# A big transposing weight load taken out of the head of a fused attention and gating kernel, with a newly searched engine order

## The chip, the cores and the metric

The kernel runs on one core of a Trainium2 chip. Times are device microseconds (us) of one execution. A run profiled by the hardware has a span, some 1.7 us shorter than its time. All runs told of here were in the fast state, at a granted TensorE clock of 0.99 to 1.00. Ratios are computed from the means: the mean time of one kernel's fast runs over that of the other's of the same rounds, so they are not quite the ratio of the medians quoted.

## The reference, cut to what matters

Two blocks on x of shape [1, 2048, 512] in bfloat16. The first is a linear attention with 32 heads, the second a gated MLP that mixes along the sequence with a 2048 x 2048 "spatial" matrix w_sp.

```
phi = lambda t: jnp.where(t > 0, t + 1, jnp.exp(t)) + 1e-06
q, k, v = split(layernorm(x) @ wqkv);  pq, pk = phi(q), phi(k)
o = (pq @ (pk^T v)) / (pq . sum(pk) + 1e-06)
h = x + o @ wo
z = gelu(layernorm(h) @ w_in);  z1, z2 = halves of z
g = w_sp @ layernorm(z2) + b_sp
out = h + (z1 * g) @ w_out
```

The matter here is the first 18 us: sixteen tiles of 128 rows of x are loaded, normalised, transposed and multiplied with the key weights. Tiles 0 to 5 are transposed by TensorE, tiles 6 to 15 by a transposing DMA on the SP queue. w_sp is needed transposed, from 118 us on.

In the kernel and its views xn is the normalised x and xnT its transpose, hn and hnT are the same for h, pk is phi(k), the z sum is the sum of pk over the rows, and wsp is w_sp transposed. x4 is the load of tiles 4 and 5, x6 that of tiles 6 and 7, and so on. SPq stands for SP's queue: the time beside it is how long an issue holds SP. The time to landing runs from the start of the issue until the data are there.

## The kernel before

The program records every operation with its dependencies; a packed string ORDER then gives the order in which each engine runs them. The loads of the head, on the two issuing queues SP and ACT:

```python
x0 = load_x("SP", 0, 1, 2150)
load_x("ACT", 1, 1, 2250)
x2 = load_x("SP", 2, 1, 2500)
load_x("ACT", 3, 1, 2500)
wk = [first_load(eng, wqkv[:, c:c + 2, D:2 * D], ...) for eng, c in (("SP", 0), ("ACT", 2))]
for n, lat, behind in ((4, 2000, x2), (6, 2200, x2), (8, 1900, wk[0]), (10, 2100, wk[0]), (12, 2300, wk[0]),
                       (14, 2500, wk[0])):
    load_x("SP", n, 2, lat, behind)          # two tiles; "behind": SP waits until that load has landed
first_load("SP", wqkv[:, :, 0:D], A_wqkv[:, 0:D], "wq", 3400)
```

The tiles from 6 on, and the spatial loads, of which the first EARLY ones are whole and stand ahead of the first transposed tile of x (cuts are marked with ...):

```python
# in k_unit(n), for i in (n, n + 1), n >= HEAD = 6
norm("ACT", xn[:, i, :], x[:, i, :], ...)
g.last = dma_t(xnT[:, :, i * P:(i + 1) * P], xn[:, i, :], f"xt{i}")   # transposing DMA on SP
...
for i, t in enumerate(order):                       # 16 row blocks of w_sp
    w = NT // 2 if EARLY <= i < NT // 2 else NT     # halves, or the whole block
    for j in range(0, NT, w):
        op = dma_t(wsp[:, j:j + w, t * P:(t + 1) * P], B_w_sp[t * P:(t + 1) * P, j * P:(j + w) * P], ...)
        ...
        if i < EARLY:
            first_xt.soft.add(op.i)                 # the load goes ahead of the first transposed tile
```

Of the kernel before, what the change touches and what calls it, by code (L numbers as in the profile page):

```python
# [8 lines left out]
ACT = mybir.ActivationFunctionType  # L9
ALU = mybir.AluOpType  # L10

P = 128
GRAN = 16
EARLY = 1
SEM_NS = 45.0
ORDER = "c-jTQ17HvU00h8Cwq47%ZQHhO+qGrewr$(CZ5wwH5gAbt9Wf9Su@D<^5Eu2800D@ED2Rr5$b~$}jl4*LqyUHz2nE3iiC_qhWJrz_NQp#9j8w>n{3w9JNQ(-ngvO|hifD@XNQl%(gMui6bjW~0NROh(gp4SL;;4eE$c!dvhAgOttSEtOsEO>Tj&A6I?kI_#D23)|fpBPrmgt4v=!-tcfm*16wy2FdXpPdSi+UJ`GAN7sXn-*oi}6^7B{+=bSc-PYiE=294rqh+XoyA_fPol{e&~-u=!i}@g3dUILzsYxn1sn#foYh6Ay|pf2#+ubi&cn#)i{b{IDz9BieU)ENCaUNMq>@uVLGOw3%X(^W?%v4<1|iU78YVH*5eGG;uKz@fg0)sp5qy2V-AL61U6tJ7GW`VU^_NpGqzwZ=3x)^VkdTCH_qWK_F+E`U@Nxa3a;WjF5n_A;U+HQ8gAh_Zr~N(;5FXjHtypN?&2OEA~+u)1Vi#2BJdF+G7{h8F`nQjKHvvF;uk*QAHLu-zTqprBPPMH49!ps!&o$9Gb*DoGNUja<1-H9G91J6H)1dqQ!@`UGdlA!3-hx8(=aX5F+DRdBQvoaOS2ZqeEfr~EJ*P$$}kwSF*|cGCkwGWb1{GkSeQjvl*L$=3Au#z*pj)~gSA<lCE13Fn3xr~m}Oa?OIe4l*qXiBmVH=}l~|co*p6$smJQgDjaZfK*^@Qcm`&J=eVLTWS%RgQgvq#t$(4dlnUc-9hbgp-TbWvEG@MgdjoUbaBiWA~*pZ#sp99#L138Gxxt%+>f-5<d={22=)L1pSjx(4+d%2HY*p1EDg4LN)sgzl1704hC<zRMaR}SM4Hc=L(Q$~$qCQai^o?%vHQ+DN0PUTiE<y9W#S3VU`K^0aZ713E9VR02z2^CXml~fs(S1Fa%9UkQ|-sKg(;Z>H?6TW2y&EkF@;6bkE25#hNj^S92<4*44A&%#4&f#3H;yg~^ah~9OF63cO;wEn9J>KU7KIBQB;yb?Q2cF}3Uf@OU=4r0xHD2c>HdQk<R|~aND^2DCPUIq1RAp7tA3o(X{$&+a)fawcHHBAeB~u%<RXep;2X#~@bygR3RRn!waD`A!g;Xtl<a6HOO+MlazT_>w;wS!NL|x`<J|+}NRAhbU5B}sY-e!CyP!xqyXh~rdRbgcXD4~8ckrFG3s;h>gD~3KZreZ0!!YP`PDvshRnBr-G`e?9ftFC6Kj%I3zhN_+hs;_2ixVmYIrfQJ7tG{|^l~!w-rYle*HCMybQzO(*qclz%G+MnBr16@ddFrkC8lzd7sC8PPC0eMpO5(Aaqyw6xrCOuOTBh~dsLfiWE!wJs+NPvltP@(U?b@Xk+N71*p}jh+L)xvK+Nb?GqCGmQ<4Wk0I;GP(qeMQY#LnfjI;RvquM4`QD@y5$itl8;rcb)A54x<Yx}&?grJK5^+`g{|O6>#=@JBt;L#6U#J<|(4(Nm@MXT8=drE_{e*B8CiS7q=!z125;*AFFk7XQ*uW%O_T6a7bjmEXZ^!*XbcabAaX2#0lehjSWda#m+{HWzR~M{q<(avn!@WJh-t7jkw-a|{=DKF4t^$8-+obP*SIF_&>!7k3HQbA88kBR6&vH*hmIbxD_ULr-!GH+OlrbSw9A8~1h}w{}IBb|qK#1o!hq_jP{{a67kkdk^#=5AiTp@nBbVIoEInS95jObS>9*M|bu{*Ku8UcMnhTR8MmUZ}Mgj^(+r}Cy(?DPxlsg@np|*kViPsvpvsqJl6}n$V)um3%%G&J<g-u)nmQfqrA+kywYpD*6SSG!F@yV+|!}F)$jF2x7E#KyxJ=~-s`==+q~U7ywkh<AMVe{ZU"


class _Op:
# [233 lines left out]
def bass_sequential_preLN__linear_attn_block__mixer_gmlp__prompt_kernel(  # L253
# [11 lines left out]
    _, S, D = A_x.shape  # L265
    F = B_w_in.shape[1]
    FH = F // 2
    H = 32
# [9 lines left out]
    g = _Prog(nc)  # L278
# [41 lines left out]
    x = g.sbuf("x", o_x, [NT, D], BF16)  # L320
    h = g.sbuf("h", o_x, [NT, D], BF16)
    xn = g.sbuf("xn", o_xn, [NT, D], BF16)
    wqkv = g.sbuf("wqkv", o_wqkv, [KD, 3 * D], BF16)
# [4 lines left out]
    pk = g.sbuf("pk", o_pk, [NT, D], BF16)  # L328
# [146 lines left out]
    def first_load(eng, dst, src, nm, lat, behind=None):  # L475
        q = queue[eng]
        op = load(eng, dst, src, nm, lat)
        op.bias = 1e6
        if q:
            op.soft.add(q[-1].i)  # L480
        if behind is not None:
            op.deps.add(behind.i)
        q.append(op)
        return op

    def load_x(eng, n, w, lat, behind=None):
        return first_load(eng, x[:, n:n + w, :], x_d[n * P:(n + w) * P, :], f"x{n}", lat, behind)

    x0 = load_x("SP", 0, 1, 2150)
    load_x("ACT", 1, 1, 2250)  # L490
    x2 = load_x("SP", 2, 1, 2500)
    load_x("ACT", 3, 1, 2500)
    wk = [first_load(eng, wqkv[:, c:c + 2, D:2 * D], A_wqkv[c * P:(c + 2) * P, D:2 * D], f"wk{c}", 3500)
          for eng, c in (("SP", 0), ("ACT", 2))]
    for n, lat, behind in ((4, 2000, x2), (6, 2200, x2), (8, 1900, wk[0]), (10, 2100, wk[0]), (12, 2300, wk[0]),
                           (14, 2500, wk[0])):
        load_x("SP", n, 2, lat, behind)
    first_load("SP", wqkv[:, :, 0:D], A_wqkv[:, 0:D], "wq", 3400)
    exp_table = g.add("ACT", lambda ac: ac.preload_act_table_set("natural_log_exp_and_others"), [], [], cost=1300)
    exp_table.soft.add(queue["ACT"][-1].i)  # L500
    exps = []
# [12 lines left out]
    def rstd(s, r, n, w, col, neg, sign=1.0):  # L514

        rr, ss = r[:, n:n + w, :], s[:, n:n + w, :]
        pool(lambda p: p.tensor_scalar(rr[:, :, 1:2], ss[:, :, col + 1:col + 2], sign, EPS_LN, op0=ALU.mult,
                                       op1=ALU.add), [ss[:, :, col + 1:col + 2]], [rr], 230)
        pool(lambda p: p.tensor_tensor(rr[:, :, 0:1], rr[:, :, 1:2],  # L519
                                       expo[:, 0:w].rearrange("p (a b) -> p a b", b=1), ALU.pow), [rr, expo], [rr],  # L520
             620 + 120 * (w - 1))
        if neg:
            for i in range(n, n + w):
                pool(lambda p, i=i: p.tensor_scalar(r[:, i, 2:3], s[:, i, col:col + 1], r[:, i, 0:1], -1.0,
                                                    op0=ALU.mult, op1=ALU.mult), [r[:, i, :], s[:, i, :]], [r[:, i, :]], 240)

    def rstd_act(s, r, n, w, col):
        rr, ve = r[:, n:n + w, :], s[:, n:n + w, col + 1:col + 2]
        act_exp(rr[:, :, 1:2], ve, ACT.Ln, 80, bias=epst[:, 1:2], extra=[epst[:, 1:2]])
        act_exp(rr[:, :, 0:1], rr[:, :, 1:2], ACT.Exp, 80, scale=-0.5)  # L530
# [22 lines left out]
    def norm(eng, dst, src, s, r, n, col, w):  # L553
        mean, rst, nmr = s[:, n, col:col + 1], r[:, n, 0:1], r[:, n, 2:3]
        if eng == "DVE":
            return dve(lambda v: v.tensor_scalar(dst, src, mean, rst, op0=ALU.subtract, op1=ALU.mult), [src, mean, rst],  # L556
                [dst], w + 460, acc=4)
        elif eng == "ACT":
            act(dst, src, ACT.Identity, w, bias=nmr, scale=rst, extra=[nmr, rst])
        else:  # L560
            pool(lambda p: p.tensor_scalar(dst, src, rst, nmr, op0=ALU.mult, op1=ALU.add), [src, nmr, rst], [dst],
                 200 + 1.5 * w)
# [43 lines left out]
    def next_pair():  # L606
        pc[0] += 1
        return PAIRS[pc[0] % 2]

    CB, first_xt, second = [4, 5, 6, 7], None, None  # L610
    HEAD, SINGLE = 6, 4
    ACTS = (1,)
    QSPLIT, KSPLIT, CACT = (6, 7), (), 2


    def k_unit(n):
        nonlocal first_xt, second
        b = next_pair()
        for i in (n, n + 1):
            if i in ACTS:  # L620
                s = st[0][:, i, :]
                act(sh_t[0], x[:, i, :], ACT.Identity, D, accum=s[:, 0:1])
                act(sh_t[1], x[:, i, :], ACT.Square, D, scale=D ** -0.5, accum=s[:, 1:2])
                moments(s, 6, D)
                rpow(s[:, 7:8], rs[0][:, i, 0:1])
            else:
                op = stats(x, 0, i)
                if i == 0:
                    second = warmup(16, 60, op)
                if n == 0:  # L630
                    rstd_act(st[0], rs[0], i, 1, 6)
        if n == 2:
            rstd_act(st[0], rs[0], n, 2, 6)
        elif n:
            rstd(st[0], rs[0], n, 2, 6, n >= HEAD)
        for i in (n, n + 1):
            norm("DVE" if n < HEAD else "ACT", xn[:, i, :], x[:, i, :], st[0], rs[0], i, 6, D)
            if n < HEAD:
                pe_transposes(xn[:, i, :], b + i % 2, xnT, i, second)
            else:  # L640
                g.last = dma_t(xnT[:, :, i * P:(i + 1) * P], xn[:, i, :], f"xt{i}")
                if i == HEAD:
                    first_xt = g.last
        for i in (n, n + 1):
            matmuls(bank(b + i % 2), [(xnT[:, c, i * P:(i + 1) * P], wqkv[:, c, D:2 * D]) for c in range(KD)])
        if n < SINGLE:
            for i in (n, n + 1):
                phi(pk[:, i:i + 1, :], b + i % 2, 1)
        else:
            phi(pk[:, n:n + 2, :], b, 2, n in KSPLIT)  # L650

        def fn(pe, i):
            inst = None
            for c in range(KD):
                inst = pe.matmul(bank(CB[c]), lhsT=xn[:, i, c * P:(c + 1) * P], rhs=pk[:, i, :],  # L655
                                 start=i == 0, stop=i == NT - 1)
            return inst
        for i in (n, n + 1):
            PE(lambda pe, i=i: fn(pe, i), [xn[:, i, :], pk[:, i, :]], [bank(b) for b in CB], KD * 216)
# [67 lines left out]
    for c in range(KD):  # L727
        b = CB[1 - c % 2]
# [100 lines left out]
    k = 0  # L829
# [190 lines left out]
```

## Time and profile before

| | before |
|---|---|
| median time, first three runs | 233.2 us (232.9 to 233.53) |
| profiled span | 231.8 us |
| TensorE busy | 224.6 us (97%) |
| first matmul on a tile transposed by DMA | 18.58 us |
| TensorE's wait for that tile | 1.20 us |

TensorE is the bound nearly everywhere, so only its gaps are worth looking for, and the lines that the prediction shows lead to the one at 17.4 to 18.6 us. Two more lines are of use. They end the views of the tiles wsp and xnT of the kernel before, and give the time from issue to landing, first for the spatial loads, then for the transposes of x:

```profile
DMA to landing us min/median/max: 3.4/4.9/9.1
```

```profile
DMA to landing us min/median/max: 2.4/2.5/4.1
```

The longest of the first, 9.1 us, is the load in the head: issued at 8.86, landed at about 17.96 us. The longest of the second is tile 7, issued at 14.47 and landed at 18.53.

### The profile page before, as it was taken

To read this page: it belongs to the slowest core of one execution; us is meant where nothing else is said; L and a number is where in the kernel's file an instruction comes from. 1 tells how busy PE (TensorE), PEld (TensorE's weight loads), DVE (VectorE), ACT (ScalarE), POOL (GpSimd) and SP (SyncE) were. 2 spreads that over 40 slices of the span, in tenths; PEclk is the share of its full clock that TensorE was granted. 3 is DMA by queue.
4 is the path that set the end of the run, shared out by engine and by line. 5 is a ranking of instruction groups with operands and counts; after the bars stand their busy time and mean duration, and the time that the engine had idled before them with its cause. 6 is when DMAs were issued, how large, how long until landed. Compare 5 with 4: busy or idle time off the path is not lost.

```text
span 231.8 us, 3231 instructions
## 1 busy us (share of the span) xinstructions
PE 224.6 (97%) x1180; PEld 112.1 (48%) x1203; DVE 161.6 (70%) x323; ACT 104.3 (45%) x193; POOL 44.2 (19%) x134
## 2 busy tenths in 40 slices
PE   8997999999999999999999999999999999999995
PEld 8543444453445443454544444444455555555452
DVE  4998755646987550237489989979795566785485
ACT  5694754399989876679862010101021211123010
POOL 3436300000466608023771000000000000000000
PEclk9999999999999999999999999999999999999999
DMA  5893259947546635968999700000000000020025
GB/s 182 263 214 70 59 138 230 315 147 181 114 89 136 117 71 121 183 126 188 185 228 197 159 3 0 0 0 0 3 0 1 0 3 0 20 72 3 0 80 191
DMA packets 58864, 23.68 MB, mean 102 GB/s; under 512 B 48480, under 2 KB 58720, under 8 KB 58848
## 3 DMA queue, kind: packets, MB, share of 16 engines
q1 hardware_dynamic: 58144, 22.88, 44.7%
q10 hardware_dynamic: 704, 0.59, 0.8%
q8 instruction: 9, 0.15, 0.3%
q14 instruction: 7, 0.06, 0.1%
HBM read 7.47 MB, written 2.10 MB: 41 GB/s over the span
## 4 chain that ended last, share of the span: by engine, by line
PE 86%; DMA 6%; ACT 3%; DVE 2%; issue 1%; SPq 0%
PE psum L402 70%; PE psum L802 6%; PE psum L655 5%; PE psum L805 4%; DMA x<-in_A_x_dram 3%; DMA xnT<-xn 2%; DMA hnT<-hn 1%; DVE st L511 1%; ACT sh L421 1%; ACT xn L421 1%; ACT e L421 0%; ACT xnT L421 0%; PE psum L751 0%; PE psum L676 0%; PE psum L720 0%
## 5 line engine op out<-in xcount | busy, mean ns | idle before, releaser
L421 ACT ACTIVATE psum<-psum 128x256 f32<-128x256 f32 (+1 forms) x33 | 14.3, 445 | 90.8 <-PE psum L402 63.1
L402 PE MATMUL psum<-wsp,z 128*128 128x512 bf16 x204 | 47.5, 379 | 0.2
L402 PEld LDWEIGHTS psum<-wsp,z 128*128 128x128 bf16 x208 | 20.4, 98 | 22.9
L402 PE MATMUL psum<-hnT,win 128*128 128x512 bf16 x108 | 25.6, 379 | 0.2
L421 ACT ACTIVATE e<-psum 128x1024 bf16<-128x1024 f32 (+1 forms) x18 | 16.7, 926 | 15.2 <-PE psum L402 14.3
L402 PE MATMUL psum<-t,s 128*128 128x512 bf16 x94 | 22.1, 379 | 0.1
L421 ACT ACTIVATE z1T<-psum 128x512 bf16<-128x512 f32 x28 | 16.6, 594 | 4.9 <-PE psum L402 4.8
L802 PE MATMUL psum<-win,hnT 128*128 128x512 bf16 x64 | 16.4, 379 | 0.4 <-DMA hnT<-hn 0.4
L402 PE MATMUL psum<-wout,z1T 128*128 128x256 bf16 (+1 forms) x82 | 16.6, 314 | 0.1
L402 PEld LDWEIGHTS psum<-hnT,win 128*128 128x128 bf16 x112 | 10.0, 98 | 13.2 <-ACT z1T L421 3.8
L402 PE MATMUL psum<-wqkv,xnT 128*128 128x512 bf16 x61 | 14.8, 380 | 1.4 <-DMA xnT<-xn 1.2
L421 ACT ACTIVATE z<-psum 128x896 bf16<-128x896 f32 x16 | 14.5, 909 | 2.9 <-PE psum L805 2.8
L402 PE MATMUL psum<-xnT,wqkv 128*128 128x512 bf16 x61 | 15.1, 379 | 0.3 <-issue 0.2
L655 PE MATMUL psum<-pk,xn 128*128 128x512 bf16 x64 | 15.3, 379 | 0.0
L402 PE MATMUL psum<-m,pqT 128*128 128x512 bf16 x62 | 14.7, 379 | 0.3 <-DVE h L776 0.2
L776 DVE SCALAR_TENSOR_TENSOR h<-psum,x 128x512 bf16<-128x512 f32 x16 | 10.8, 688 | 5.2 <-PE psum L402 5.1
L402 PEld LDWEIGHTS psum<-t,s 128*128 128x128 bf16 x96 | 9.4, 98 | 10.3
L582 DVE TENSOR_SCALAR e<-e 128x1024 bf16<-128x1024 bf16 (+1 forms) x18 | 7.1, 397 | 9.1 <-ACT e L421 9.0
L805 PE MATMUL psum<-win,hnT 128*128 128x384 bf16 x64 | 13.0, 326 | 0.0
L924 DVE TENSOR_TENSOR u<-psum,bsp 128x512 bf16<-128x512 f32 x16 | 11.0, 687 | 2.8 <-PE psum L402 2.7
L556 DVE TENSOR_SCALAR z<-z,st,rs 128x896 bf16<-128x896 bf16 x16 | 7.2, 493 | 7.3 <-POOL rs L519 7.3
L511 DVE BATCH_NORM_STATS2 st<-x 128x6 f32<-128x512 bf16 x15 | 9.7, 677 | 3.6 <-DMA x<-in_A_x_dram 3.6
(113 smaller groups left out, 349.3 us busy)
## 6 DMA issues: line engine op xcount, KB each, us to landing
r<-rcp SPq DMA_DIRECT2D x16, 128.0 KB, 2.6
out_dram<-h SPq DMA_DIRECT2D x15, 128.0 KB, 1.8
win<-in_B_w_in_dram SPq DMA_DIRECT2D x2, 896.0 KB, 6.6
x<-in_A_x_dram SPq DMA_DIRECT2D x6, 256.0 KB, 4.5
wqkv<-in_A_wqkv_dram SPq DMA_DIRECT2D x2, 512.0 KB, 5.2
wout<-in_B_w_out_dram SPq DMA_DIRECT2D x1, 896.0 KB, 7.2
wo<-in_A_wo_dram SPq DMA_DIRECT2D x1, 512.0 KB, 8.3
bsp<-in_B_b_sp_dram SPq DMA_DIRECT2D x1, 512.0 KB, 5.1
```

The source lines that it names most:

```text
L402: inst = pe.matmul(out_ap, lhsT=a, rhs=b, start=start and i == 0, stop=stop and i == len(pairs) - 1, **kw)
L421: return g.add("ACT", lambda ac: ac.activation(out_ap, in_ap, func, **kw), [in_ap, *extra], [out_ap] + ([accum] if accum is not None else []),
L511: dve(lambda v: v.bn_stats(s[:, 0:6], src[:, n, :]), [src[:, n, :]], [s[:, 0:6]], D)
L556: return dve(lambda v: v.tensor_scalar(dst, src, mean, rst, op0=ALU.subtract, op1=ALU.mult), [src, mean, rst], [dst], w + 460, acc=4)
L582: dve(lambda v: v.tensor_scalar(e, e, 1.0, EPS_PHI, op0=ALU.min, op1=ALU.add), [e], [e], w * GW, acc=4)
L655: inst = pe.matmul(bank(CB[c]), lhsT=xn[:, i, c * P:(c + 1) * P], rhs=pk[:, i, :], start=i == 0, stop=i == NT - 1)
L776: dve(lambda v, n=n, b=b, s=s: v.scalar_tensor_tensor(h[:, n, :], bank(b), 1.0, x[:, n, :], op0=ALU.mult, op1=ALU.add, accum_out=s[:, 0:1] ...
L802: pe.matmul(bank(b), lhsT=hnT[:, c, n * P:(n + 1) * P], rhs=win2[:, c, 0:GW], start=c == 0, stop=c == KD - 1)
L805: inst = pe.matmul(bank(b + 1, F2), lhsT=hnT[:, c, n * P:(n + 1) * P], rhs=win2[:, c, GW:FH], start=c == 0, stop=c == KD - 1)
L924: dve(lambda v: v.tensor_tensor(t, bank(b), add, ALU.add), [bank(b), add], [t], GW, ps=True)
```

## The change

The intent is to keep the spatial load out of the head, to chain x8 to x14 behind the ACT half of the key weights in place of the SP half, and to search the engine order again with landing times as measured. The diff, with the packed orders, and options that are off (ND, LEAD and lead), cut:

```diff
-EARLY = 1
+EARLY = 0
-ORDER = "c-jTQ17HvU00h8C..."
+ORDER = "c-jrogMttU00qE@..."
...
-    for n, lat, behind in ((4, 2000, x2), (6, 2200, x2), (8, 1900, wk[0]), (10, 2100, wk[0]), (12, 2300, wk[0]),
-                           (14, 2500, wk[0])):
+    first_load("SP", wqkv[:, 0:2, D:2 * D], A_wqkv[0:2 * P, D:2 * D], "wka", 4200)
+    wk = first_load("ACT", wqkv[:, 2:4, D:2 * D], A_wqkv[2 * P:4 * P, D:2 * D], "wkb", 4400)
+    for n, lat, behind in ((4, 3000, x2), (6, 3200, x2), (8, 3850, wk), (10, 4000, wk), (12, 4200, wk), (14, 4400, wk)):
         load_x("SP", n, 2, lat, behind)
```

With EARLY = 0 the first row block is loaded as two halves, late, so there are 24 spatial issues in place of 23.

More of the change, by code (lines that the diff above doesn't have):

```diff
@@ L13 @@
 GRAN = 16
-EARLY = 1
+EARLY = 0
 SEM_NS = 45.0
-ORDER = "c-jTQ17HvU00h8Cwq47%ZQHhO+qGrewr$(CZ5wwH5gAbt9Wf9Su@D<^5Eu2800D@ED2Rr5$b~$}jl4*LqyUHz2nE3iiC_qhWJrz_NQp#9j8w>n{3w9JNQ(-ngvO|hifD@XNQl%(gMui6bjW~0NROh(gp4SL;;4eE$c!dvhAgOttSEtOsEO>Tj&A6I?kI_#D23)|fpBPrmgt4v=!-tcfm*16wy2FdXpPdSi+UJ`GAN7sXn-*oi}6^7B{+=bSc-PYiE=294rqh+XoyA_fPol{e&~-u=!i}@g3dUILzsYxn1sn#foYh6Ay|pf2#+ubi&cn#)i{b{IDz9BieU)ENCaUNMq>@uVLGOw3%X(^W?%v4<1|iU78YVH*5eGG;uKz@fg0)sp5qy2V-AL61U6tJ7GW`VU^_NpGqzwZ=3x)^VkdTCH_qWK_F+E`U@Nxa3a;WjF5n_A;U+HQ8gAh_Zr~N(;5FXjHtypN?&2OEA~+u)1Vi#2BJdF+G7{h8F`nQjKHvvF;uk*QAHLu-zTqprBPPMH49!ps!&o$9Gb*DoGNUja<1-H9G91J6H)1dqQ!@`UGdlA!3-hx8(=aX5F+DRdBQvoaOS2ZqeEfr~EJ*P$$}kwSF*|cGCkwGWb1{GkSeQjvl*L$=3Au#z*pj)~gSA<lCE13Fn3xr~m}Oa?OIe4l*qXiBmVH=}l~|co*p6$smJQgDjaZfK*^@Qcm`&J=eVLTWS%RgQgvq#t$(4dlnUc-9hbgp-TbWvEG@MgdjoUbaBiWA~*pZ#sp99#L138Gxxt%+>f-5<d={22=)L1pSjx(4+d%2HY*p1EDg4LN)sgzl1704hC<zRMaR}SM4Hc=L(Q$~$qCQai^o?%vHQ+DN0PUTiE<y9W#S3VU`K^0aZ713E9VR02z2^CXml~fs(S1Fa%9UkQ|-sKg(;Z>H?6TW2y&EkF@;6bkE25#hNj^S92<4*44A&%#4&f#3H;yg~^ah~9OF63cO;wEn9J>KU7KIBQB;yb?Q2cF}3Uf@OU=4r0xHD2c>HdQk<R|~aND^2DCPUIq1RAp7tA3o(X{$&+a)fawcHHBAeB~u%<RXep;2X#~@bygR3RRn!waD`A!g;Xtl<a6HOO+MlazT_>w;wS!NL|x`<J|+}NRAhbU5B}sY-e!CyP!xqyXh~rdRbgcXD4~8ckrFG3s;h>gD~3KZreZ0!!YP`PDvshRnBr-G`e?9ftFC6Kj%I3zhN_+hs;_2ixVmYIrfQJ7tG{|^l~!w-rYle*HCMybQzO(*qclz%G+MnBr16@ddFrkC8lzd7sC8PPC0eMpO5(Aaqyw6xrCOuOTBh~dsLfiWE!wJs+NPvltP@(U?b@Xk+N71*p}jh+L)xvK+Nb?GqCGmQ<4Wk0I;GP(qeMQY#LnfjI;RvquM4`QD@y5$itl8;rcb)A54x<Yx}&?grJK5^+`g{|O6>#=@JBt;L#6U#J<|(4(Nm@MXT8=drE_{e*B8CiS7q=!z125;*AFFk7XQ*uW%O_T6a7bjmEXZ^!*XbcabAaX2#0lehjSWda#m+{HWzR~M{q<(avn!@WJh-t7jkw-a|{=DKF4t^$8-+obP*SIF_&>!7k3HQbA88kBR6&vH*hmIbxD_ULr-!GH+OlrbSw9A8~1h}w{}IBb|qK#1o!hq_jP{{a67kkdk^#=5AiTp@nBbVIoEInS95jObS>9*M|bu{*Ku8UcMnhTR8MmUZ}Mgj^(+r}Cy(?DPxlsg@np|*kViPsvpvsqJl6}n$V)um3%%G&J<g-u)nmQfqrA+kywYpD*6SSG!F@yV+|!}F)$jF2x7E#KyxJ=~-s`==+q~U7ywkh<AMVe{ZU"
@@ new lines @@
+ORDER = "c-jrogMttU00qE@tj)G<d$VoZwz=81ZQHhO+jiZ}FHA&4MpVQ_03sm@q9HnBASPlVHsT;Y5+E1yAUE;?AVR?ihTssAAQ6%x8ImIfLLem)BOmf36$+pb(xN;nq5_(r5*i^M5+XIypdbn(9Wo$20+9(tkP$^u3|UbbRgf8t(G*!w71>Y&*-;$b(G?}o1Km&(&Cnbz(E>fu3%$_?)leO6kOMVQ8@131rBDZTF%G3s24gTDV^I(Fu?$PF6wA>Tt&tODQ4a0V4ihjDp%D&~F$sOq5B)I!)6fA^&;SiF5Q8usQ*jU-(Fq~30xPi^s}LURFc?7?f<qXA;aG!_7=_U|j3YRTV+ex?IDxP@j?U<U8JLOrSb$krh?6*tp%{j>SdTL}g=ct<7kG-<n1e-FjE&fU9oUY!n1@Z+j4jxMz1WFe*o|{Ii+$LS1K5gfxQZ({j|;eno4AC_xQ1J}jvIJ|H+YNJxQ)BGk9)X-hX~FG2*Hqyz()vRM83m&JjN6Jzz2N7PkhEV{KCioOJnd0zT+$YAvD7<6vHwmW04HU@cfOajKb)Q#K=s=)XdEM%)@BR!UD|8QjE(ujLmpV!#~K%g3L!VEz>bQGcX&oGY4}rBmbf_#hNV3I?TmjjL!rt$Arwp++4yI3}hh|W)T);2^M2r)?!PpVR!aoYnEXmCT4loV{I<xQdVGbmSl4EU~jf!3aw>*Hef?GVntSBWmaKhR%cZvWimElGbUkjrsNi;)*klcGN#d9Ze<Ei;Rvo{8@6R14&_vi<Ua1_Fs4*`rP51OV?8xxbJk!6rB!B4XJ7VXf3{<Lc3?*iU?&dbAkN?ccIJ9+U{}^x5F4lq2eTW8a5&Q`i!v&cvMZ}{D4TLCr}AhTb1A>ha1=*#49D^y$8jdlGOvy>pSH1}?(irBRX~MwmxWbC#Z*)!R9vN0QpZ?YWmHyISWa(vl}}h+*Z7uy_>|B1m$SH$vpJq~c!<k6mn*o5^EinUc#rqFkdrx)=XjnM_<-~IklT5jk9dMBxr!J0j@P+^J9(0)xQjP<lehSuhk2UM`GPO`im!Q_|G1eS_>mALHB=)t)&eeK6E#&cHCGF@R5G<vYqe2ZwNra_P)BuAXLV6mRZt~;;a67FH-=XP1y>ctQwUX6NX1tTediDUq!pluiloT8#8CRh$K1`;yvzhjs6?u%%8I5ss;20wuDY73SqiOB45P40tRxDi7>cP_N~+%srznc8IEt#cs-@4Is%h$@APvwE%~3ZEQ(tx03=P#h_0Vb!)F6$}NDWti4OUO}(`fZlZ;jF#jn_tv(F9G@SWVY#t<`!>(q@g*d@a;cP1Zrp)jB2h0!`5})z$`W(jslqVlCHJEzt_C)HZF`4(-+|?Nl=F(mw6i0Ugybom5Jn(rKk~BA?YE9oG@<(HWgkVjos=pVN8e_61$mMP1b;rST12R|;RzHQm)c#rJLP)h*rELp@LeCv<v$)F*w>BRy6+KhbkN)k|e`9zW9?CGlsyR%*Y{D}B{BWpY}-(|di_PyJ8^|JE=4Q9i?eC1>?N1#@uIb{L0sNQZJbM{sy&b~a~sL1%FRM|6O5IFchfs-ruv^E;<wIi{nykfS+<3%i(eIj#d;#6?})C0x&OJlXYK#*N(AO<dL`-OLT$)D2w9E!^DY-O{bx+P&P{ZQR!F-OhbHz!lxkeO<|wUD^}f-veF6<vhqiuId^d><X^t>aOWpp5)rD<00<gq3-04?&`Yk;;EkI=^pNp9_A6A?M<HHnV#a&p5@No>@6PUIiBnJp67*L?4@4dMPA}%?%^@s>h50dabDr^UhP$0>vdl54Zf++4&gicpxAz^ZXWAx?&+1D;CNo+jo$7Z-sxT5?f(EflF2O"
@@ L478, in first_load @@
         op.bias = 1e6
-        if q:
+        if q and q[-1] is not behind:
             op.soft.add(q[-1].i)
@@ L487, in load_x @@
         return first_load(eng, x[:, n:n + w, :], x_d[n * P:(n + w) * P, :], f"x{n}", lat, behind)
-    x0 = load_x("SP", 0, 1, 2150)
-    load_x("ACT", 1, 1, 2250)
-    x2 = load_x("SP", 2, 1, 2500)
-    load_x("ACT", 3, 1, 2500)
-    wk = [first_load(eng, wqkv[:, c:c + 2, D:2 * D], A_wqkv[c * P:(c + 2) * P, D:2 * D], f"wk{c}", 3500)
-          for eng, c in (("SP", 0), ("ACT", 2))]
-    for n, lat, behind in ((4, 2000, x2), (6, 2200, x2), (8, 1900, wk[0]), (10, 2100, wk[0]), (12, 2300, wk[0]),
-                           (14, 2500, wk[0])):
+    load_x("SP", 0, 1, 2150)
+    load_x("ACT", 1, 1, 2300)
+    x2 = load_x("SP", 2, 1, 2300)
+    load_x("ACT", 3, 1, 2550)
+    first_load("SP", wqkv[:, 0:2, D:2 * D], A_wqkv[0:2 * P, D:2 * D], "wka", 4200)
+    wk = first_load("ACT", wqkv[:, 2:4, D:2 * D], A_wqkv[2 * P:4 * P, D:2 * D], "wkb", 4400)
+    for n, lat, behind in ((4, 3000, x2), (6, 3200, x2), (8, 3850, wk), (10, 4000, wk), (12, 4200, wk), (14, 4400, wk)):
         load_x("SP", n, 2, lat, behind)
-    first_load("SP", wqkv[:, :, 0:D], A_wqkv[:, 0:D], "wq", 3400)
+    first_load("SP", wqkv[:, :, 0:D], A_wqkv[:, 0:D], "wq", 3500)
     exp_table = g.add("ACT", lambda ac: ac.preload_act_table_set("natural_log_exp_and_others"), [], [], cost=1300)
@@ L611, in bass_sequential_preLN__linear_attn_block__mixer_gmlp__prompt_kernel @@
     HEAD, SINGLE = 6, 4
-    ACTS = (1,)
+    ACTS, ND, LEAD, lead = (1,), (), 0, []
     QSPLIT, KSPLIT, CACT = (6, 7), (), 2
@@ L618, in k_unit @@
         b = next_pair()
+        first = len(g.ops)
         for i in (n, n + 1):
@@ L631, in k_unit @@
                     rstd_act(st[0], rs[0], i, 1, 6)
+        if n == 2 and LEAD:
+            for op in g.ops[first:]:
+                if op.eng == "DVE":
+                    op.soft.add(lead[LEAD - 1].i)
         if n == 2:
@@ L634, in k_unit @@
         elif n:
-            rstd(st[0], rs[0], n, 2, 6, n >= HEAD)
+            rstd(st[0], rs[0], n, 2, 6, n >= HEAD or n in ND or n + 1 in ND)
         for i in (n, n + 1):
-            norm("DVE" if n < HEAD else "ACT", xn[:, i, :], x[:, i, :], st[0], rs[0], i, 6, D)
+            lead.append(norm("DVE" if n < HEAD and i not in ND else "ACT", xn[:, i, :], x[:, i, :], st[0], rs[0], i, 6, D))
             if n < HEAD:
@@ L647, in k_unit @@
             for i in (n, n + 1):
-                phi(pk[:, i:i + 1, :], b + i % 2, 1)
+                phi(pk[:, i:i + 1, :], b + i % 2, 1, i in KSPLIT)
         else:
```

## The prediction

> **What bounds the kernel now.** I read the views in this order: busy time and the 40 slices on the page, the chain of work that ended last, TensorE's waits, and then the time line of the first 30 us, engine by engine.
>
> ```profile
> PE 224.6 (97%) x1180; PEld 112.1 (48%) x1203; DVE 161.6 (70%) x323; ACT 104.3 (45%) x193; POOL 44.2 (19%) x134
> PE   8997999999999999999999999999999999999995
> PEclk9999999999999999999999999999999999999999
> ```
>
> TensorE is busy for 97% of the 231.8 us span, at full clock. Only the first slices and the last one are below 9 tenths. So nothing that frees another engine helps by itself: a gain must be a gap of TensorE that closes. The page's 97% counts each matmul with its modelled end and so hides small gaps; the chain, which counts them from start to start, is the better view (start us, us, what):
>
> ```profile
> 4.00 3.56 DMA x<-in_A_x_dram
> ...
> 10.53 0.57 DVE pk L587
> ...
> 14.40 0.07 ACT e L421
> 14.47 4.06 DMA xnT<-xn
> 18.53 0.05 issue
> 18.58 0.61 PE psum L402 x2
> ...
> 118.81 10.74 PE psum L402 x49
> 129.55 0.05 issue
> 129.60 10.74 PE psum L402 x49
> ```
>
> From 118.81 us a block of 49 recorded matmuls takes 10.74 us, then comes the next: 10.74/49 is 0.219 us, or 0.215 us if one record in fifty is missing, which is what eight 512-column matmuls in 1.73 us elsewhere in the chain give (0.216 us). From there to 229.2 us TensorE has no gap, and the view of its waits finds none in that stretch. The same count from 18.58 to 48.25 us (128 matmuls of 0.216 us, plus 0.97 and 0.79 us for the two groups of the z sum: 29.4 of 29.7 us) leaves 0.3 us. What can be won lies in the head, up to 18.58 us, and between 48 and 66 us. TensorE's own waits of some size (waiter, releaser, us in total, times, longest):
>
> ```profile
> PE psum L402 <- DMA xnT<-xn: 1.2, 1, 1.2
> PE psum L594 <- POOL warm L439: 1.0, 1, 1.0
> PE psum L802 <- DMA hnT<-hn: 0.4, 1, 0.4
> PE psum L402 <- ACT m L421: 0.3, 1, 0.3
> PE psum L402 <- DVE h L776: 0.2, 1, 0.2
> ```
>
> The largest is the first transposed activation tile. Why it comes late is in the time line of the SP queue and of ACT:
>
> ```profile
> 8.35 0.47 SPq L432 DMA_DIRECT2D wqkv<-in_A_wqkv_dram  x1
> 8.86 5.56 SPq L435 DMA_TRANSPOSE wsp<-in_B_w_sp_dram  x1
> 14.47 3.48 SPq L435 DMA_TRANSPOSE xnT<-xn  x2
> 12.41 0.80 ACT L421 ACTIVATE xn<-x,rs 128x512 bf16<-128x512 bf16 x1
> 13.59 0.81 ACT L421 ACTIVATE xn<-x,rs 128x512 bf16<-128x512 bf16 x1
> ```
>
> The first tile to be transposed by DMA (number 7) is normalised by ACT at 12.41+0.80 = 13.21 us, but SP is inside the issue of one big transposing load of the spatial weights from 8.86 to 14.42 us, and sends tile 7 only at 14.47 us. It lands 4.06 us later, at 18.53; the ten transposes of this kind take 2.5 us in the median, so this one also lost time on the way.
>
> **What the Trainium skill says.** The page "DMA: Bandwidth & Descriptors", in "Anatomy of one DMA — SWDGE (gpsimd) path", says that a wait for a semaphore is made by the issuing sequencer and not by the DMA engines, so an instruction queued behind a long issue waits for it. The trace agrees: tile 7 goes out 0.05 us after the 5.56 us issue ends, 1.26 us after its data were there. The same page, in "Issuing engines are not separate DMA queues", says that all DMAs run on the same 16 engines and interleave. That agrees too: between 8 and 16 us the mean DMA share is 1.00 and the last x loads and the query weights land 5.0 and 6.2 us after issue, against 2.6 us for the very first x loads. "TensorE: Matmul & The Clock Gate", in "Wait — 56ns, not 53.3ns?", gives 215.7 ns from start to start for 512 columns at full clock; the 0.216 us above is the same.
>
> **The change, part by part.**
>
> 1. *The spatial-weight load leaves the head.* I unpacked the new engine order and read it against the old kernel's list of operations. On SP, the load that stood between the query weights and tile 7 now stands after the fifth transposed tile of h (some 70 us), as two half loads; there are 24 such issues instead of 23. In the head this takes away 5.56 us of SP issue and the traffic with it. Tile 7 can go out at 13.25 us and, with the usual 2.5 us, lands at about 15.8; tile 6, ready at 14.40, at about 17.0 (estimates). TensorE wants them after the last head matmuls on the fourth k tile. Those wait for VectorE, which is busy without a gap from 7.58 us and finishes that tile at 15.55+0.69 = 16.24 us; the four matmuls start at 16.30 and the next could start at 16.30+4x0.216 = 17.2 us. It started at 18.58. **So 1.4 us goes, all of the wait**, with about 1.4 us to spare on the DMA side. VectorE is the bound behind it, and the new order does the same VectorE work up to that point, so no more than this is won there.
>
> 2. *Does the gain survive to 48 us?* The second pair (8, 9) is normalised between 15.81 and 17.31 us, would be issued at about 16.7 and 17.9 and land by 19.2 and 20.4. TensorE, moved 1.4 us forward, wants tile 8 at 17.2+4x0.86 = 20.7 us and tile 9 at 21.5. The third pair had 27.2-1.4 = 25.8 us as its old need moved forward and its statistics are put earlier in the new VectorE order. It holds, and the train to 48 us moves as a whole.
>
> 3. *x4 to x15.* Tiles 4 and 6 are chained behind x2 as before. Tiles 8 to 14 now wait for the ACT half of the key weights in place of the SP half; the two landed 4.8 and 4.7 us after issues at 1.72 and 1.71 us, so this moves four issues by 0.1 us. VectorE has no gap between 7.58 and 17.75 us in which to feel that. Worth 0. The changed landing times are inputs of the search and cost nothing themselves.
>
> 4. *ACT in the first 10 us.* The reciprocal root of tile 0 starts before the second sum of tile 1, but ends behind it, and the copies of tiles 0 to 3 change places. By the durations (0.6 us each) the fourth k matmul group still ends near 11.4 us, and the transposes after it wait for VectorE at 11.02+0.41. Worth 0, at most 0.3 us either way.
>
> 5. *48 to 119 us.* Here the load returns. Taking the operations of TensorE from 48.3 us at their start-to-start costs gives 118.8 us for the first spatial matmul; the trace has it at 120.3. So 1.5 us of gaps lie in this stage: m copied by ACT, the first hnT, a bank freed by VectorE. The new order issues the second transposed h tile earlier and moves one projection group (0.86 us) behind the first spatial matmuls, which changes the sum by nothing. A search may win a part of the 1.5 us; I count 0.2 us. The spatial transposes of the first pass: ten halves stand behind the last h tile, 10x1.35 = 13.5 us plus 0.6 for the bias. If that tile goes out by 98 to 103 us as before, they are issued by 112 to 117 us and land some 5 us later, against a need at about 118.5 to 122 us: just enough. I take off 0.2 us for this.
>
> Sum: -1.4 + 0 + 0 - 0.2 + 0.2 = -1.4 us. The time before is 233.2 us, so 231.8 us, and a profiled span of 230.4.
>
> **Rivals.** (a) *The gain is taken back by a late spatial load.* TensorE would wait at 118 to 124 us for tiles that before were partly in place at 18 and 40 us. For it: VectorE is busy 18.8 of 20 us from 120 to 140, so a late first sum of spatial weights is not recovered. Against it: before, the first such sum runs at 124.0 us, long after its tiles; eight full-width transposes of the second pass lie between and are needed 40 us later. If it happened: 232.5 to 235 us. (b) *The head is bound by VectorE at later tiles too, so that TensorE waits again at tiles 4 to 9 and less than 1.4 us survives.* For it: its gap-free stretch. Against it: in the old trace its work on tiles 4 and 5 ended at 17.83 us, and TensorE, moved forward, wants them at 18.9. But the new order puts 0.9 us of statistics ahead of them (18.8 us), which is on the edge. Would give 232.2 to 232.9. (c) *The fresh order closes the gaps of 48 to 66 us as well*, 1.4+1.5: 230.3 us at best. For it: the search had measured landing times; against it: ACT is busy 11.6 of 12 us from 48 to 60, so there is little to reorder. (d) *The early DMA traffic did not matter and tile 7 still takes 4 us*: 13.25+4.06 = 17.3 us, which costs 0.1 us.
>
> **Range and chances.** Main line 231.8; rival (b) or a mild (a) gives 232.2 to 233, (c) down to 230.3. Eight in ten: 230.9 to 232.9. Two per cent is 4.7 us: faster would need all gaps of the head and the middle and more, slower a new wait of 4.7 us in a stage of 70 us with slack. Chances: faster 0.02, same 0.96, slower 0.02.
>
> **What would show it.** Right: no spatial issue on SP before 60 us; the first xnT transpose issued near 13.25 us and landed by 16; TensorE's wait for xnT gone, and its first matmul on the DMA-made tiles near 17.2 us; the z sum near 44 us in place of 45.45; the first spatial matmul near 118. Wrong at step 1: the transposes still issue or land late, or TensorE starts earlier than 17.1. Wrong at step 2: new TensorE waits for pk, xnT or ACT between 18 and 45 us. Wrong at step 5: waits for hnT or wsp after 65 us, or first spatial matmuls not 1.4 us earlier than before.

## The result, and the profile after

The changed kernel takes 232.37 us in the median of 6 runs (232.18 to 232.89), the kernel before 233.35 us (232.9 to 233.56). The ratio is 0.9963 (0.9948 to 0.9978): within 2%, in the range, and clear of noise. The gain was to be 1.4 us; this measurement shows 0.98 us between the medians, while the profiled spans differ by 1.3 us (231.8 and 230.5). Two more measurements of the same kernel, below, give ratios of 0.9947 and 0.995, or 1.38 and 1.13 us between medians.

The page of the changed kernel, busy time, TensorE's slices and its clock:

```profile
PE 224.0 (97%) x1180; PEld 111.4 (48%) x1203; DVE 160.7 (70%) x323; ACT 104.0 (45%) x193; POOL 45.0 (20%) x134
PE   8899999999899999999999999999999999999995
PEclk9999999999999999999999999999999999999999
```

The shares look the same; a gap of 1.2 us in 231 does not show in them. It does show in TensorE's waits (waiter, releaser, us in total, times, longest):

```profile
PE psum L593 <- POOL warm L439: 1.0, 1, 1.0
PE psum L755 <- DVE pqT L584: 0.8, 1, 0.8
PE psum L569 <- DVE xn L555: 0.7, 3, 0.3
PE psum L402 <- ACT m L421: 0.3, 1, 0.3
```

The wait for xnT is gone and none for hnT or wsp has come. The chain that ended last, in the head (start us, us, what):

```profile
7.37 0.42 DVE xn L555
...
8.29 3.40 PE psum L402 x15
11.69 0.30 PE psum L569 x4
12.00 0.86 PE psum L659 x4
12.86 0.26 PE psum L569 x4
13.12 1.79 PE psum L402 x8
14.91 2.59 PE psum L659 x12
17.50 0.43 PE psum L402 x2
```

Before, the chain passed here through the loads of x, VectorE, ACT and the transpose; now, from 8.29 us to the end of the head, it is TensorE without a break. SP's time line after:

```profile
8.53 0.47 SPq L432 DMA_DIRECT2D wqkv<-in_A_wqkv_dram  x1
13.36 5.90 SPq L435 DMA_TRANSPOSE xnT<-xn  x4
```

Tile 7 goes out at 13.36 us, 1.1 us earlier than before, and lands 2.9 us later, at 16.26 us, 1.1 us before TensorE takes it up; no other transpose of x takes longer. The first spatial load goes out at 73.09 us.

From the first matmul on a DMA-made tile to the first spatial matmul it was 101.74 us (18.58 to 120.32) and is 100.85 us (17.34 to 118.19); the new order moved one projection group of 0.86 us behind the latter. So nothing was won or lost from 18 to 120 us: 0.03 us. The gaps changed all the same: the waits for hnT and h of the kernel before (0.4 and 0.2 us) are gone, and the wait of 0.8 us for pqT, at 63.42 us, is new.

### The profile page after: what moved, and what is told of

Same layout as the page of the kernel before. It is cut to its first block, busy times and chain, and to the rows that moved or that the text cites. A ratio compares the mean times of both kernels' runs of the same rounds, so it can differ in the third digit from the quotient of the medians.

```text
span 230.5 us, 3228 instructions
## 1 busy us (share of the span) xinstructions
PE 224.0 (97%) x1180; PEld 111.4 (48%) x1203; DVE 160.7 (70%) x323; ACT 104.0 (45%) x193; POOL 45.0 (20%) x134
## 3 DMA queue, kind: packets, MB, share of 16 engines
HBM read 7.47 MB, written 2.10 MB: 42 GB/s over the span
## 4 chain that ended last, share of the span: by engine, by line
PE 90%; ACT 3%; POOL 2%; issue 1%; DMA 1%; DVE 1%
PE psum L402 72%; PE psum L659 6%; PE psum L806 6%; PE psum L809 5%; DMA x<-in_A_x_dram 1%; POOL rs L550 1%; ACT e L421 1%; POOL st L536 1%; ACT sh L421 1%; PE psum L755 0%; ACT m L421 0%; PE psum L724 0%; PE psum L680 0%; PE psum L569 0%; POOL st L534 0%
## 5 line engine op out<-in xcount | busy, mean ns | idle before, releaser
L822 DVE BATCH_NORM_STATS2 st<-z 128x6 f32<-128x512 bf16 x9 | 6.2, 691 | 9.8 <-ACT z L421 9.8
L555 DVE TENSOR_SCALAR hn<-h,st,rs 128x512 bf16<-128x512 bf16 x16 | 6.0, 400 | 9.6 <-POOL rs L546 9.0
```

The source lines that it names most:

```text
L555: return dve(lambda v: v.tensor_scalar(dst, src, mean, rst, op0=ALU.subtract, op1=ALU.mult), [src, mean, rst], [dst], w + 460, acc=4)
L822: dve(lambda v, n=n, s=s: v.bn_stats(s[:, 0:6], z2[:, n, 0:GW]), [z2[:, n, 0:GW]], [s[:, 0:6]], GW)
```

## The experiments

Twelve kernels were run; all gave correct results. The first four ran on one chip and share the runs of the kernel before, and so do the next three and the four after them; the twelfth ran alone.

### 1. Only the load moved, the old order kept

To the kernel before:

```diff
-EARLY = 1
+EARLY = 0
 # in schedule(), after ORDER is unpacked: 606 and 607 are the two halves, 608 the next spatial load
+        ids = [i + (i > 606) for i in ids if i != 606]
+        k = ids.index(608)
+        ids[k:k] = [606, 607]
```

> The kernel before, with only the spatial-weight load taken out of the head and put, as two half loads, behind the output weights (33 us); every other instruction in the old order. Theory (the whole gain is the head load leaving; the new search adds nothing): TensorE's wait of 1.2 us for xnT is gone, its first matmul on the DMA-made tiles is at 17.2 to 17.4 us, time ratio 0.994 to 0.997, the same as the change. Rival (the gain needs the newly searched order): ratio above 0.998, or a new wait after 30 us that takes the gain back; the rest of the weights are issued about 3 us later here.

Measured: 233.9 us against 233.59, ratio 1.0014 (0.9994 to 1.0034). The wait for xnT was gone, yet nothing was won. TensorE's time line of this run, in the stage of the output projection:

```profile
52.89 0.38 PE L405 MATMUL psum<-wo,kvm 128*128 128x512 bf16 x1 [0.84 <-DMA wo<-in_A_wo_dram]
```

The two half loads, put behind the output weights at 33 us, pushed the projection weights wo back: they were issued at 43.37 us and took 9.4 us to land (in the kernel before, at 41.49 us and 8.3 us), and TensorE waited for them.

### 2. The new order with the load put back in the head

To the changed kernel:

```diff
-EARLY = 0
+EARLY = 1
+        ids = [i - (i > 607) for i in ids if i not in (606, 607)]
+        ids.insert(ids.index(109), 606)        # 109 is the transpose of tile 7
```

> The changed kernel with the single big spatial load put back between the query weights and tile 7, every other instruction in the new order. Theory: the wait for xnT of 1.2 to 1.4 us returns and the ratio to the kernel before is 0.999 to 1.002. Rival (the new order itself is worth something): ratio 0.997 or below with the wait present.

Measured: 233.59 us, ratio 1.0 (0.9978 to 1.0021). TensorE's time line:

```profile
18.27 1.90 PE L404 MATMUL psum<-wqkv,xnT 128*128 128x512 bf16 x7 [0.64 <-DMA xnT<-xn]
```

The wait is back, though at 0.64 us it is half of what was expected. In this profile tile 7 landed 0.3 us earlier than in the kernel before (18.22 against 18.53 us), and VectorE started on x4 0.25 us later, so that TensorE came later to the wait. The load landed at 8.80+8.9 = 17.7 us, and tile 7, 0.5 us after it. With the load in the head the new order is worth nothing that these runs can see.

### 3. The changed kernel again

> The changed kernel unaltered, as the yardstick on this chip and for the spread from run to run. Ratio 0.9963 was measured (interval 0.9948 to 0.9978), while the two profiled spans differ by 1.3 us, which would be 0.9944. If the true gain is the span's 1.3 us, this run gives 0.994 to 0.995; if the measured 0.86 us is the true one, 0.996 to 0.997. The first x tile landed 0.2 us later in the profile of the change; if that is chance, it should vary from run to run in either kernel.

Measured: 232.21 us (232.08 to 232.79), ratio 0.9947 (0.9926 to 0.9968). The same kernel as a yardstick, whose expectation was:

> The changed kernel unaltered, yardstick for the other runs of this call; ratio 0.9945 to 0.9965 expected from its two earlier measurements (0.9963 and 0.9947).

It gave 232.36 us, ratio 0.995 (0.9932 to 0.9968). The three measurements lie between 0.98 and 1.38 us of gain.

### 4. ACT's head order as it was

To the changed kernel; 36 and 33 are the second sum of tile 1 and the root of tile 0, the other pairs are copies of tiles:

```diff
+        for op, at in ((36, 33), (65, 46), (68, 49)):
+            ids.remove(op)
+            ids.insert(ids.index(at), op)
```

> The changed kernel with ACT's order in the first 10 us as it was: the second sum of tile 1 ahead of the reciprocal root of tile 0, and the copies of tiles 0 to 3 in the old sequence. Theory (the new ACT order delays tile 1's normalisation by 0.4 us and TensorE's head matmuls with it, so part of the expected 1.4 us was lost there): tile 1 normalised near 6.9 in place of 7.37 us, first key matmul near 7.9 in place of 8.29, and 0.1 to 0.3 us faster than the changed kernel in the same call. Rival (VectorE is the bound of the head at 16.24 us whatever ACT does): first key matmul earlier, but the first matmul on DMA-made tiles unchanged near 17.3 us and the time equal within 0.1 us.

Measured: 232.16 us against 232.21 for run 3, equal. From VectorE's start on x0, as it lands, to the first key matmul it takes 4.47 us here and 4.73 us in run 3 (8.06-3.59 and 8.12-3.39), so the new ACT order does cost 0.26 us; but the first matmul on DMA-made tiles moves only from 17.19 to 17.11 us. The rival holds: something behind it sets the time.

### 5. Traffic without the long issue

To the changed kernel, behind the query weights on SP, a plain load of 2 MB into a region that is overwritten later:

```diff
+    load("SP", wsp[:, 0:4, :], B_w_sp[0:4 * P, :], "traffic", 6000)
```

> The changed kernel with an extra plain load of 2 MB into a region that is overwritten later, at the place on SP where the spatial load stood. Its issue should take some 0.5 us, so SP is free for tile 7 at 13.3 us, but the DMA queue is full until about 16 to 18 us (2 MB at the 320 GB/s seen in this stretch is 6.5 us from 9.5 us). Theory A (tile 7 came late because its bytes stood behind the spatial load's in the queue): tile 7 is issued near 13.3 us yet lands only about when the extra load does, 16.5 to 18 us, and TensorE waits up to 0.7 us for it. Theory B (the late issue on SP was the cause, as the prediction told it): tile 7 lands by 16.5 us and there is no wait.

SP's time line, and then TensorE's:

```profile
8.71 0.56 SPq L434 DMA_DIRECT2D wsp<-in_B_w_sp_dram  x1
13.42 8.06 SPq L437 DMA_TRANSPOSE xnT<-xn  x5
```

```profile
20.82 3.12 PE L404 MATMUL psum<-wqkv,xnT 128*128 128x512 bf16 x8 [3.25 <-DMA xnT<-xn]
```

The times to landing, of the loads into wsp and then of the transposes of x, of which the longest are the extra load and tile 7:

```profile
DMA to landing us min/median/max: 3.4/4.5/11.5
```

```profile
DMA to landing us min/median/max: 2.4/2.6/7.4
```

SP was free after 0.56 us and sent tile 7 at 13.42 us, on time. Still TensorE waited 3.25 us for it. The extra load took 11.5 us to land, so until 20.2 us, and tile 7 followed it by 0.6 us. Theory A holds; my estimate of 6.5 us for the 2 MB forgot the x loads and the query weights ahead of it in the queue, so the dose was too large. One thing is not told apart: all of this went through SP's queue. No run sends the load or the transpose through the other one, so whether the order within the queue makes tile 7 late, or the traffic on the 16 DMA engines whatever the queue, is not tested.

The time was 237.77 us (235.92 to 238.39), ratio 1.0166 (1.0113 to 1.0219): some 5.4 us above the changed kernel for a wait of 3.25. The windows view (the stretch, its length, busy time of each engine, then granted clock, DMA share and GB/s) shows the rest:

```profile
20.00:22.00 2.00, 1.18 (x4) 0.46 (x5) 0.80 (x3) 0.00 (x0) 1.50 (x5) 0.84 1.21 243
22.00:24.00 2.00, 2.00 (x6) 0.76 (x5) 0.00 (x0) 0.03 (x1) 0.11 (x1) 0.50 0.09 18
24.00:26.00 2.00, 2.00 (x9) 0.82 (x8) 0.93 (x2) 2.00 (x3) 0.00 (x0) 0.81 0.00 0
```

After the wait TensorE was granted half its clock for a while (0.84, 0.50, 0.81). Weighted over these six microseconds that is (0.16+0.50+0.19)x2 = 1.7 us lost. In three of the four runs the mean clock was 0.992 or 0.993 and the spans were 235.8 to 236.7 us; in the fourth it was 1.0 and the span 234.2 us.

### 6. The late issue without traffic

To the changed kernel; 106 is the normalisation of tile 6:

```diff
+                if i == 7:
+                    g.last.deps.add(106)
```

> The changed kernel in which tile 7's transpose is made to wait for the normalisation of tile 6 too, so that it is issued at about 14.5 us as in the kernel before, without any spatial traffic. Theory A (traffic in the queue was the cause): it lands 2.5 us later, near 17.1 us, tile 6 near 18.3, and TensorE loses 0 to 0.2 us. Theory B (the late issue was the cause): the wait of about 1.2 us returns and the time is that of the kernel before.

SP's and TensorE's time lines:

```profile
15.02 5.20 SPq L435 DMA_TRANSPOSE xnT<-xn  x4
```

```profile
17.82 2.10 PE L402 MATMUL psum<-wqkv,xnT 128*128 128x512 bf16 x8
```

And the transposes' times to landing:

```profile
DMA to landing us min/median/max: 2.4/2.5/2.9
```

Tile 7 was issued at 15.02 us, 6.85 us after VectorE's start on x4, where the kernel before has 6.89 us. It landed 2.5 us later, and TensorE did not wait. The time was 232.53 us, ratio 0.9958 (0.9941 to 0.9975), that of the change. The late issue alone costs nothing measurable.

### 7. Only the chaining of x8 to x14

To the kernel before: `wk[0]` becomes `wk[1]` in the four places, and the ACT loads stand earlier in the list to satisfy it (no engine's own order changes).

> The kernel before with one edit: tiles 8 to 14 of x wait for the ACT half of the key weights in place of the SP half. Expected 0: four issues move by 0.1 us or less, VectorE works without a gap meanwhile; ratio 0.999 to 1.001. The rival, that this chaining carries part of the gain, needs 0.998 or below.

Measured: 233.74 us (232.25 to 234.82), ratio 1.0003 (0.996 to 1.0046). No effect is seen, but with four runs and this spread, one below 0.4% could hide. In its profile the load landed at 9.13+9.5 = 18.63 us and tile 7 at 15.10+4.06 = 19.16 us, again 0.5 us behind it.

### 8. The load moved, the projection weights first, the old order kept

As run 1, with one more line: wo (231) is issued right behind the value weights (230).

```diff
-        ids = [i + (i > 606) for i in ids if i != 606]
+        ids = [i + (i > 606) for i in ids if i not in (606, 231)]
         k = ids.index(608)
         ids[k:k] = [606, 607]
+        ids.insert(ids.index(230) + 1, 231)
```

> The run that moved only the load, in the old order, gained nothing (ratio 1.0014) although its wait for xnT was gone; its profile had a new TensorE wait of 0.8 us for the output projection weights, which its two half loads had pushed back. Here those weights are issued ahead of the spatial halves, nothing else changes. Theory (the gain in the head is real and independent of the search, and the load's new place took it back): no wait for those weights, ratio 0.994 to 0.997. Rival (the old order cannot use the earlier head): ratio 0.999 or above without that wait.

Measured: 232.07 us (231.87 to 232.81), ratio 0.9943 (0.9922 to 0.9965), without a wait for wo. The old order with two moves gives all that the new search gives. It is 1.8 us faster than run 1. In the two profiles the stretch from the z sum to the first spatial matmul took 75.89 us in run 1 (44.87 to 120.76) and 74.63 us here (44.02 to 118.65), 1.26 us of it; the rest is in run 1's x4, which VectorE could start on only at 8.37 us, against 7.53. Whether x4 was that late in run 1's other five runs was not recorded (the profiled one, at 233.96 us, is close to their median), and why it should be is open.

### 9 and 10. x4 earlier

To the changed kernel: x4 does not wait for x2; in run 9 it is also issued ahead of the key weights.

```diff
-    for n, lat, behind in ((4, 3000, x2), ...
+    for n, lat, behind in ((4, 3000, None), ...
+        op = load_x("SP", n, 2, lat, behind)
+        if n == 4:                             # run 9 only
+            op.soft = {x2.i}
 # in schedule(), run 9 only: 19 is the SP half of the key weights, 21 is x4
+        ids.remove(21)
+        ids.insert(ids.index(19), 21)
```

> The changed kernel with x4 issued right behind x2 and ahead of the SP half of the key weights, without waiting for x2 to land. In the profiles so far VectorE starts on x4 between 7.47 and 8.37 us and, without the spatial load, TensorE's first matmul on DMA-made tiles follows 9.64 to 9.65 us later in every one. Theory (the landing of x4 varies from run to run and passes straight into the time): VectorE no longer waits for x4, and the time is 0.1 to 0.4 us below the changed kernel of this call with a narrower spread. Rival: the key weights or x0 to x3 land later by as much and TensorE waits for those: equal or slower.

> The changed kernel with x4 issued without waiting for x2, but behind the key weights as before (2.2 us in place of 4.0 to 4.3). Theory: x4 lands by about 7 us, no VectorE wait for it, 0.1 to 0.4 us below the changed kernel of this call; as good as the run with x4 ahead of the key weights. Rival: the early loads share the DMA engines and x0 to x3 land later: equal or slower.

Run 9: 232.28 us (232.2 to 232.31), ratio 0.9945 (0.9928 to 0.9962). Run 10: 232.48 us (232.31 to 232.78), ratio 0.9955 (0.9938 to 0.9973). The yardstick has 232.36 us. No faster, but run 9's spread is 0.11 us, against 0.47 us for the yardstick. That fits x4's landing being a part of the spread, though six runs of each do not prove it. Run 10, in whose profile x4 landed no earlier than in the yardstick's, has 0.47 us too.

### 12. Both

Run 8 with the x4 edit of run 9.

> The old order with the spatial load moved behind the projection weights (ratio 0.9943 so far) and, besides, x4 issued ahead of the SP half of the key weights without waiting for x2, which left the changed kernel's median where it was and narrowed its spread from 0.5 to 0.1 us. Theory (x4's landing is a part of the spread, and in the old order of ACT it can be the bound of the head): ratio 0.992 to 0.9945, spread below 0.4 us. Rival (the early load of x4 delays others by as much): ratio 0.9945 or above.

Measured: 231.78 us (231.7 to 232.09) against 233.58, ratio 0.9916 (0.9878 to 0.9954; a run of 236.23 us among those of the kernel before lowers it, and the medians give 0.9923). It is the best of all and beats both kernels, by 1.8 us and by some 0.5 us. It was run at another time. Part of that may be chance: it was not run beside run 8.

### What the runs have in common

For each profile: when VectorE starts on x4, when TensorE starts on the transposes of tile 4, and its first matmul on DMA-made tiles (us; TensorE's and VectorE's time lines).

| run | load in head | x4 starts | tile 4 transposed | first DMA-made tile | last less third |
|---|---|---|---|---|---|
| before | yes | 7.58 | 11.48 | 18.58 | 7.10 |
| 7, chain only | yes | 7.93 | 11.84 | 19.21 | 7.37 |
| 2, load back | yes | 7.83 | 11.73 | 18.27 | 6.54 |
| after | no | 7.70 | 11.60 | 17.34 | 5.74 |
| 3, after | no | 7.54 | 11.45 | 17.19 | 5.74 |
| 4, ACT head | no | 7.47 | 11.37 | 17.11 | 5.74 |
| 1, load moved | no | 8.37 | 12.28 | 18.02 | 5.74 |
| 6, delay | no | 8.17 | 12.08 | 17.82 | 5.74 |
| 8, wo first | no | 7.53 | 11.43 | 17.17 | 5.74 |
| 9, x4 ahead | no | 7.69 | 11.59 | 17.33 | 5.74 |
| 12, both | no | 7.38 | 11.32 | 17.05 | 5.73 |

(Runs 10 and 11 have 5.73 too. Run 5, with its extra load, has 9.16.) Without the load the stretch is 5.74 us whatever else is done: 24 matmuls of 0.216 us and two groups of transposes of some 0.28 us, packed. With it, it is 0.8 to 1.6 us longer. What precedes it is 3.9 us from the start on x4, and x4's start wanders between 7.4 and 8.4 us. In most profiles that start follows x4's landing. Not in the first profile of the changed kernel: there x4 landed at 4.14+3.3 = 7.4 us, and VectorE, which had waited 0.18 us for a root that GpSimd makes, was busy with the last of the first four tiles until 7.7 us. In runs 5, 9 and 12 too x4 had landed, 0.2 to 0.6 us before VectorE took it up.

## Why the prediction was right or wrong

**The time and the range: right, in part by luck.** 231.8 us was predicted and 232.37 measured, in the range of 230.9 to 232.9; the profiled span was to be 230.4 and is 230.5. The change takes away the long issue and its bytes together, so the number came out right although the prediction mostly blamed the wrong one of the two.

**Step 1, the size: right; the cause: wrong.** By the table, 7.10 us became 5.74: 1.36 us, the predicted 1.4. But the step put the delay down to SP "inside the issue of one big transposing load", with some time "also lost on the way". Runs 5 and 6 turn this round: a late issue without traffic costs nothing, traffic without a late issue makes TensorE wait. Tile 7's bytes stood in the queue behind the spatial load's. They landed some 0.5 to 0.6 us after it in each of the three profiles with the spatial load in the head (before, runs 2 and 7) and after the extra load in run 5, though their issue began 3.5 to 6.8 us before that load had landed. The 5.56 us of the issue are no fixed cost of the load either: the eight other whole row blocks of the same kernel, issued from 109.53 us on, held SP for 1.7 to 3.1 us each. Why the one in the head took so much longer was not tested. The prediction had the figures to see it (8.86+9.1 and 14.47+4.06) and did not set them side by side. The Trainium skill has the rule on the page already cited, "DMA: Bandwidth & Descriptors", in "Queues, rings and completion order": on each DMA engine descriptors are consumed in ring order. The landings, 0.5 to 0.6 us behind the load in four profiles, agree with it. One sign was missed narrowly: tile 7 was to land by 16 us, at about 15.8, and landed at 16.26, which left 1.1 us to spare in place of 1.4.

**Rival (d) did not come.** It supposed that the early traffic did not matter and that tile 7 would take 4.06 us from its earlier issue too, and cost 0.1 us. Without the load it took 2.9 us. With a larger load in front, run 5 shows 7.4 us from issue to landing for an issue made on time: there the earlier issue won nothing.

**"VectorE is the bound behind it": half right.** TensorE was to start near 17.2 us, and did at 17.34, 0.12 us of it because VectorE started on x4 0.12 us later. But from the transposes of tile 4 on TensorE itself is packed, and the fourth tile of VectorE is done just in time. What VectorE and x4's landing set is the start of that packed stretch.

**Step 2, right.** No TensorE wait for xnT, pk or ACT came between 18 and 45 us. Rival (b) did not happen. The z sum came at 43.33 us and not near 44, because the new order puts it ahead of a group of four key-value matmuls (0.86 us), which the prediction overlooked.

**Step 3, right as far as the runs can tell** (run 7: 1.0003, give or take 0.4%). The four issues moved by 0.18 us (6.40 to 6.58), not by 0.1.

**Step 4, right.** "At most 0.3 us either way": 0.26 us from x0 to the first key matmul, and nothing in the time (run 4). But the prediction did not see that the new ACT order can make VectorE late for x4, as in the changed kernel's first profile; how much of the 0.12 us above is due to it, and how much to x0, which VectorE started on 0.2 us later there, is open.

**Step 5, right in sum.** The 48 to 119 us stage moved by 0.03 us; the search won nothing there in sum, so neither the 0.2 us nor rival (c) came, and the late spatial tiles of rival (a) were in time. That there was room for harm is shown by run 1, in which two half loads at a worse place cost a wait of 0.84 us for other weights.

**What the search was worth.** Nothing that the runs can see: run 2 has the new order and no gain, run 8 the old order and all the gain. The prediction's sum of steps 3 to 5, zero, says the same.

**Why the medians show less than the spans.** Three measurements gave 0.98, 1.38 and 1.13 us. The wandering of x4's start is wide enough, and run 9, which takes x4's wait away, has the narrowest spread; that this is the whole reason is argued, not shown.

## What to carry to other kernels

Before a late transfer is put down to its late issue, add its time to landing to its issue time and do the same for what is ahead of it in the queue: if the one lands just behind the other, suspect the bytes in front: here moving the issue alone cost or won nothing (runs 5 and 6). A big load that is not needed for a hundred microseconds belongs where no short transfer on TensorE's path, and no other weight that is due soon, follows it in the same queue. When a change bundles one such move with a new search of the order, run each half alone: here the move carried all of it.

## What the Trainium skill lacked or had wrong

- "DMA: Bandwidth & Descriptors", "Queues, rings and completion order", gives the ring order but no figure for what a short transfer pays behind a long one. Here a transpose of one tile, 2.5 us in the median, took 4.06 us behind a transposing load of a 128 x 2048 block and 7.4 us behind a plain load of 2 MB, in both cases ending about 0.6 us after it.
- The same page has cycle counts of the sequencer for transposing instructions, but none for these sizes, and does not say that the issue time can vary by three times for one size. Here a block of 128 x 2048 held SP for 5.4 to 5.9 us in the head of three profiles, and for 1.7 to 3.1 us from 109.53 us on in the kernel before; a tile of 128 x 512 held it for 1.2 to 2.2 us.
- "TensorE: Matmul & The Clock Gate", "What's actually happening", says that the clock halves after at least one idle window of about 3.4 us and that the window runs freely. In the profile of run 5 the clock halves at 21.34 us and is full again at 24.76, 3.42 us later, which agrees with the length. But TensorE had worked 0.52 of the 3.41 us before 21.34, so in this one profile a wait of 3.25 us was enough, without a window that is idle throughout. Some 1.7 us were lost, and in one of the four runs the mean clock stayed at 1.
- No page says by how much the first loads' landing wanders from run to run: x4, issued at 4.0 to 4.3 us behind x2, landed between 7.4 and 8.4 us in these profiles.
